# k and q of tiles 9 to 23 transposed by DMA instead of by TensorE, and identity matmuls in TensorE's waits of the first four tiles

## The chip, the cores and the metric

The kernel runs on one core of one Trainium2 chip. The metric is device time in microseconds (us); the kernel before takes 236.11 us, the median of three runs (236.11 to 236.44).

## The reference

Two blocks stand one behind the other. The first is a causal linear attention with a decay per head (4 batches, 8 heads, 768 positions, head size 64), given in blocks of 64 positions:

```python
for b in range(nb):
    ...
    intra = np.einsum('bhic,bhjc->bhij', qb, kb) * Dmask[None]
    intra = np.einsum('bhij,bhjd->bhid', intra, vb)
    inter = np.einsum('bhid,bhde->bhie', qb * lam_pow[None], kv_state)
    out[:, :, sl] = intra + inter
    ...
    kv_state = lam_block[None, :, None, None] * kv_state + np.einsum('bhsd,bhse->bhde', kb_dec, vb)
```

The heads are put side by side to rows of 512. The second block normalizes each row and adds a two-layer network of width 2048:

```python
xn = (x - mu) / np.sqrt(var + 1e-06) * g_ln
ch = np.maximum(xn @ w_ch1, 0.0) @ w_ch2
return (x + ch)
```

Inputs and outputs are float32; the kernel multiplies in bf16.

## The kernel before, in words

The 3072 rows are cut into 24 tiles of 128 positions, six to a batch. The decay is taken out of the mask: q is scaled by lam^(i+1) and v by lam^-(i+1), so that the scores need only a triangular mask, and the state between tiles is multiplied by lam^128. All eight heads of a tile are worked on together, two heads ("a pair") to 128 columns.

A tile goes through these steps.

- `p0` (L293): three loads from HBM on SP's queue (`load_tile`, L56, 256 KB each, in runs of 256 bytes), then three GpSimd instructions: `kb` (k cast to bf16, L138), `qb` and `vb` (q and v scaled, L144 and L146).
- `p1` (L149): TensorE transposes k and q, four 128x128 transposes each (`tk` L153, `tq` L162). ScalarE copies `tk` from PSUM in two halves of 64 partitions (L155, L156) into `kTp`, a buffer whose other halves were zeroed at the start; `qT` is copied by ScalarE for tiles 0 to 3 and by VectorE afterwards.
- `p2` (L170): k transposed times v for the next state (`pk`, L177), its sum with the old state on VectorE (`Stmp`, L184) and the decay on GpSimd (`Sn`, L185); then the scores `sc` (L192), eight 128x128 matmuls whose contraction runs over 128 rows, half of them the zeros of `kTp`, and the mask on VectorE (`mA`, L194).
- `p3` (L198): the output `po` (eight matmuls L203, and four with the state, L207), copied by ScalarE to `x` (L210), its statistics (L212, L214) and the centred, scaled `xc` (L216) on VectorE.
- `p4` (L219): `xc` transposed into `xT`, by TensorE for tiles 0 to 7 (L234) and by a DMA transpose on SP's queue from tile 8 on (L227).
- The two layers work on groups of tiles, of sizes 2, 2, 1, 1, 2, 2, 3, 4, 4, 3 (L288). `m1` (L258) multiplies by the first weights, ScalarE applies the ReLU (L261); `m2` (L271) multiplies by the second weights, VectorE adds x (L282), and SP's queue stores the tile (L284).

Every engine, and SP's queue, works in the order in which the code issues its instructions. Up to group 3 the order is written out by hand (L319 to L370: a list of `units` of the layers, and in `after` the attention steps that follow each). From group 4 on a loop (L388) goes through the units of the layers and hands out attention steps at an even pace, so that the last tile of a group has had its `p4` six units before the group begins. A `round_of(j)` (L306) holds the steps that are taken together. The weights come as eight DMAs issued by GpSimd, `w1` in four (L75) and `w2` in four (L78); the four of `w2` stand in GpSimd's queue behind `vb` of tile 4, which waits for that tile's last load. That load is itself held back by a memset on GpSimd (L63, `after_pool`).

PSUM has two banks `aux` (`tk`, `tq`, `pk`, `xt`), two for scores, one for `po` and three `mm` for the layers.

Of the kernel before, what the change touches and what calls it, by code (L numbers as in the profile page):

```python
# [16 lines left out]
def kernel(  # L17
# [94 lines left out]
    kTp = []  # L112
    for i in range(2):
        kt = const.tile([128, NP, 2, 128], BF16, name=f"kTp{i}")
        nc.vector.memset(kt, 0.0)
        kTp.append(kt)
# [13 lines left out]
    st = {}  # L130
# [4 lines left out]

    def in_k(t, eng):
        kb = wk.tile([128, H, D], BF16, tag="kb", bufs=4, name="kb")
        (eng.copy if eng is nc.scalar else eng.tensor_copy)(kb, qkv_in[t]["k"])  # L138
        st[t] = dict(kb=kb)

    def in_qv(t):
        f = qkv_in.pop(t)
        qb = wk.tile([128, H, D], BF16, tag="qb", name="qb")
        nc.gpsimd.tensor_tensor(qb, f["q"], lam_q[:, :, None].to_broadcast([128, H, D]), op=ALU.mult)  # L144
        vb = wk.tile([128, H, D], BF16, tag="vb", bufs=4, name="vb")
        nc.gpsimd.tensor_tensor(vb, f["v"], lam_v[:, :, None].to_broadcast([128, H, D]), op=ALU.mult)  # L146
        st[t].update(qb=qb, vb=vb)

    def p1(t):  # L149
        s = st[t]  # L150
        tk = ps.tile([128, NP, 128], BF16, tag="aux", bufs=2, name="tk")
        for p in range(NP):
            nc.tensor.transpose(tk[:, p, :], s["kb"][:, 2 * p:2 * p + 2, :], ident)  # L153
        kT = kTp[t % 2]
        nc.scalar.copy(kT[0:64, :, 0, :], tk[0:64, :, :])  # L155
        nc.scalar.copy(kT[64:128, :, 1, :], tk[64:128, :, :])  # L156
        if t < 4:
            tq = ps.tile([128, NP, 128], BF16, tag="mm", bufs=3, name="tq")
        else:
            tq = ps.tile([128, NP, 128], BF16, tag="aux", bufs=2, name="tq")  # L160
        for p in range(NP):
            nc.tensor.transpose(tq[:, p, :], s["qb"][:, 2 * p:2 * p + 2, :], ident)  # L162
        qT = wk.tile([128, NP, 128], BF16, tag="qT", name="qT")
        if t < 4:
            nc.scalar.copy(qT, tq)
        else:
            nc.vector.tensor_copy(qT, tq)  # L167
        s["kT"], s["qT"] = kT, qT

    def p2(t):  # L170
        s = st[t]
        c = t % nb
        s["S"] = state.get("S") if c > 0 else None
        if c < nb - 1:
            pk = ps.tile([128, NP, 128], F32, tag="aux", bufs=2, name="pk")
            for p in range(NP):
                nc.tensor.matmul(pk[:, p, :], lhsT=s["kb"][:, 2 * p:2 * p + 2, :], rhs=s["vb"][:, 2 * p:2 * p + 2, :],  # L177
                                 start=(p == 0), stop=(p == NP - 1), skip_group_check=True)
            Sn = wk.tile([128, NP, 128], BF16, tag="S", name="Sn")
            if c == 0:  # L180
                nc.vector.tensor_tensor(Sn, pk, lamC, op=ALU.mult)
            else:
                tmp = wk.tile([128, NP, 128], F32, tag="Stmp", bufs=2, name="Stmp")
                nc.vector.tensor_tensor(tmp, pk, state["S"], op=ALU.add)  # L184
                nc.gpsimd.tensor_tensor(Sn, tmp, lamC, op=ALU.mult)  # L185
            state["S"] = Sn
        mA = wk.tile([128, H, 128], BF16, tag="mA", name="mA")
        for half in range(2):
            sc = ps.tile([128, H // 2, 128], F32, tag="sc", bufs=2, name="sc")
            for i in range(H // 2):  # L190
                h = half * (H // 2) + i
                nc.tensor.matmul(sc[:, i, :], lhsT=s["kT"][:, h // 2, h % 2, :], rhs=s["qT"][:, h // 2, :],  # L192
                                 start=(i == 0), stop=(i == H // 2 - 1), skip_group_check=True)
            nc.vector.tensor_tensor(mA[:, half * (H // 2):(half + 1) * (H // 2), :], sc,  # L194
                                    tril[:, None, :].to_broadcast([128, H // 2, 128]), op=ALU.mult)
        s["mA"] = mA

    def p3(t):  # L198
# [3 lines left out]
        for h in range(H):  # L202
            nc.tensor.matmul(po[:, h, :], lhsT=s["mA"][:, h, :], rhs=s["vb"][:, h, :],  # L203
# [12 lines left out]
        nc.vector.scalar_tensor_tensor(xc, in0=x, scalar=mv[:, 0:1], in1=g_row, op0=ALU.subtract, op1=ALU.mult)  # L216
# [71 lines left out]
    sizes = [2, 2, 1, 1, 2, 2, 3, 4, 4, 3]  # L288
# [4 lines left out]
    def p0(t):  # L293
        for n in {4: (), 5: (8, 9)}.get(t, (t + 4,)):
            if n < NT:
                load_tile(n)
        in_k(t, nc.gpsimd)
        in_qv(t)
# [20 lines left out]
    for t in range(2):  # L319
        in_k(t, nc.vector)  # L320
        in_qv(t)
# [3 lines left out]
    run((p1, 0), (p2, 0), (p1, 1), (p3, 0))  # L325
    in_k(2, nc.scalar)
    in_qv(2)
    load_w1(0)
    run((p2, 1), (p1, 2), (p3, 1))
    in_k(3, nc.scalar)  # L330
    in_qv(3)
    load_w1(1)
    load_tile(4, after_pool=True)
    run((p2, 2), (p4, 0), (p1, 3), (p3, 2))
    load_w1(2)
    load_w1(3)
    run((p2, 3), (p4, 1), (p0, 4))
# [36 lines left out]
    for j in range(8, NT + 2):  # L374
# [51 lines left out]
```

## Time and profile before

| | |
|---|---|
| median of three runs | 236.11 us |
| the profiled execution, its own time | 235.61 us |
| its span, first to last instruction | 233.9 us |
| TensorE matmuls (PE) busy | 212.4 us, 91% of the span |
| weight loads (PEld) | 136.8 us |
| VectorE (DVE) | 113.3 us, 48% |
| ScalarE (ACT) | 114.3 us, 49% |
| GpSimd (POOL) | 90.1 us, 39% |
| mean granted TensorE clock | 0.981 |
| read from HBM, written | 27.53 MB, 6.29 MB |

In the lines of the profile PE is TensorE's matmuls, PEld its weight loads, SPq the queue of SyncE, which issues the loads, the stores and the DMA transposes. A line of a timeline begins with the start and the length in us. A line of the waits gives the total, the number of times and the longest. The chain is the work that ended last, followed back from the end, each piece released by the one ahead of it. A matmul's duration includes its way through the pipeline, so matmuls that follow each other overlap; what one costs is the distance to the next start.

### The profile page before, as it was taken

How to read it: one execution, taken by the hardware profiler on the slowest of the kernel's cores; microseconds unless marked ns; L12 is line 12 of the kernel's file. 1: busy time of each engine (PE TensorE's matmuls, PEld its weight loads, DVE VectorE, ACT ScalarE, POOL GpSimd, SP SyncE). 2: the span in 40 equal slices, each digit the busy share in tenths (PEclk: the TensorE clock that was granted, in tenths of full speed). 3: DMA queues.
4: the chain of work that ended last, by engine and by line, in shares of the span. 5: the costliest groups of instructions: out<-in, count | busy, mean ns of one | idle time of the engine just before them, and what ended most of it. 6: DMA issues, size and time to landing. Idle time of an engine off the chain costs nothing.

```text
span 233.9 us, 4503 instructions
## 1 busy us (share of the span) xinstructions
PE 212.4 (91%) x1792; PEld 136.8 (58%) x1792; DVE 113.3 (48%) x219; ACT 114.3 (49%) x222; POOL 90.1 (39%) x103
## 2 busy tenths in 40 slices
PE   0664899999999899989999999999999999999992
PEld 0453879644977596579567655555554544456540
DVE  3459530334665567868776656653573223220021
ACT  5765486421546465367437832678213664017400
POOL 2659526216834667952746940633220000000000
PEclk9997799999999999999999999999999999999998
DMA  6998996999999999999999903310011200411012
GB/s 125 221 225 113 221 176 89 182 217 205 225 209 300 204 242 227 209 210 243 168 249 229 160 3 112 93 22 3 34 66 59 67 0 3 125 60 39 3 66 70
DMA packets 91717, 32.02 MB, mean 137 GB/s; under 512 B 84272, under 2 KB 88624, under 8 KB 91696
## 3 DMA queue, kind: packets, MB, share of 16 engines
q1 hardware_dynamic: 87328, 27.53, 58.7%
q0 software_dynamic: 4224, 4.19, 11.3%
q8 instruction: 14, 0.23, 0.4%
q14 instruction: 7, 0.06, 0.1%
q10 hardware_dynamic: 144, 0.00, 0.0%
HBM read 27.53 MB, written 6.29 MB: 145 GB/s over the span
## 4 chain that ended last, share of the span: by engine, by line
PE 70%; DMA 15%; SPq 4%; POOL 4%; DVE 3%; ACT 2%; issue 1%; DVEq 0%; ACTq 0%
PE pm L271 30%; PE pm L258 28%; DMA vin<-in_v_dram 7%; DMA w<-in_moe_w_ch_dram 6%; SPq L65 4%; PE sc L192 3%; PE po L203 2%; DMA xT<-xc 2%; PE tq L162 2%; PE po L207 1%; PE tk L153 1%; POOL vb L146 1%; PE pk L177 1%; DVE xc L216 1%; POOL w L78 1%
## 5 line engine op out<-in xcount | busy, mean ns | idle before, releaser
L258 PE MATMUL pm<-xT,w 128*128 128x256 bf16 (+3 forms) x640 | 90.4, 294 | 1.5 <-DMA xT<-xc 0.8
L271 PE MATMUL pm<-w,hT 128*128 128x512 bf16 x384 | 88.6, 379 | 0.1
L261 ACT ACTIVATE hT<-pm 128x512 bf16<-128x512 f32 (+1 forms) x104 | 58.2, 565 | 44.5 <-PE pm L258 43.6
L258 PEld LDWEIGHTS <-w 128*128 128x128 bf16 x640 | 56.2, 98 | 25.4 <-DMA xT<-xc 1.0
L271 PEld LDWEIGHTS <-hT 128*128 128x128 bf16 x384 | 36.3, 98 | 38.0 <-issue 0.4
L185 POOL TENSOR_TENSOR Sn<-Stmp,lamC 128x512 bf16<-128x512 f32 x16 | 20.4, 1273 | 60.9 <-DVE Stmp L184 60.9
L212 DVE BATCH_NORM_STATS2 stats<-x 128x6 f32<-128x512 f32 x24 | 16.7, 694 | 43.6 <-ACT x L210 43.5
L282 DVE SCALAR_TENSOR_TENSOR o<-pm,rstd,x 128x512 f32<-128x512 f32 (+1 forms) x25 | 18.0, 725 | 33.6 <-PE pm L271 33.3
L194 DVE TENSOR_TENSOR mA<-sc,tril 128x512 bf16<-128x512 f32 x48 | 30.7, 681 | 1.3 <-PE sc L192 1.3
L144 POOL TENSOR_TENSOR qb<-qin,lam_q 128x512 bf16<-128x512 f32 x24 | 25.6, 1066 | 13.7 <-DMA qin<-in_q_dram 13.6
L155 ACT COPY kTp<-tk 64x512 bf16<-64x512 bf16 x24 | 13.7, 572 | 31.4 <-PE tk L153 31.4
L146 POOL TENSOR_TENSOR vb<-vin,lam_v 128x512 bf16<-128x512 f32 x24 | 25.5, 1062 | 3.9 <-DMA vin<-in_v_dram 2.8
L210 ACT COPY x<-po 128x512 f32<-128x512 f32 x24 | 14.0, 585 | 16.0 <-PE po L207 12.5
L216 DVE SCALAR_TENSOR_TENSOR xc<-x,mv,g_row 128x512 bf16<-128x512 f32 x24 | 20.7, 862 | 0.9
L192 PE MATMUL sc<-qT,kTp 128*128 128x128 bf16 x192 | 16.4, 234 | 0.3 <-ACT kTp L156 0.2
L167 DVE COPY qT<-tq 128x512 bf16<-128x512 bf16 x20 | 8.4, 419 | 15.2 <-PE tq L162 15.1
L153 PE MATMUL tk<-ident,kb 128*128 128x128 bf16 x96 | 10.0, 231 | 6.1 <-DVE kb L138 5.5
L138 POOL CAST kb<-kin 128x512 bf16<-128x512 f32 x20 | 13.2, 661 | 5.7 <-DMA kin<-in_k_dram 5.5
L192 PEld LDWEIGHTS <-kTp 128*128 128x128 bf16 x192 | 13.5, 106 | 1.6 <-ACT kTp L156 0.4
L156 ACT COPY kTp<-tk 64x512 bf16<-64x512 bf16 x24 | 13.9, 581 | 0.6
L162 PE MATMUL tq<-ident,qb 128*128 128x128 bf16 x96 | 9.7, 227 | 3.9 <-POOL qb L144 3.5
L203 PEld LDWEIGHTS <-mA 128*128 128x128 bf16 x192 | 9.0, 99 | 6.7 <-DVE mA L194 3.4
(45 smaller groups left out, 112.5 us busy)
## 6 DMA issues: line engine op xcount, KB each, us to landing
kin<-in_k_dram SPq DMA_DIRECT2D x24, 256.0 KB, 4.9
qin<-in_q_dram SPq DMA_DIRECT2D x24, 256.0 KB, 5.0
vin<-in_v_dram SPq DMA_DIRECT2D x24, 256.0 KB, 5.4
out_dram<-o SPq DMA_DIRECT2D x23, 256.0 KB, 2.5
w<-in_moe_w_ch_dram POOLq DMA_DIRECT2D x8, 512.0 KB, 8.0
g_row<-in_moe_g_ln_dram SPq DMA_DIRECT2D x1, 256.0 KB, 5.0
xT<-xc SPq DMA_TRANSPOSE x16, 3.2
out_dram<-o SPq DMA_DIRECT2D x2, 128.0 KB, 1.7
```

Source lines behind the costliest of these rows:

```text
L144: nc.gpsimd.tensor_tensor(qb, f["q"], lam_q[:, :, None].to_broadcast([128, H, D]), op=ALU.mult)
L146: nc.gpsimd.tensor_tensor(vb, f["v"], lam_v[:, :, None].to_broadcast([128, H, D]), op=ALU.mult)
L162: nc.tensor.transpose(tq[:, p, :], s["qb"][:, 2 * p:2 * p + 2, :], ident)
L185: nc.gpsimd.tensor_tensor(Sn, tmp, lamC, op=ALU.mult)
L192: nc.tensor.matmul(sc[:, i, :], lhsT=s["kT"][:, h // 2, h % 2, :], rhs=s["qT"][:, h // 2, :], start=(i == 0), stop=(i == H // 2 - 1), skip ...
L194: nc.vector.tensor_tensor(mA[:, half * (H // 2):(half + 1) * (H // 2), :], sc, tril[:, None, :].to_broadcast([128, H // 2, 128]), op=ALU.mult)
L212: nc.vector.bn_stats(stats, x)
L216: nc.vector.scalar_tensor_tensor(xc, in0=x, scalar=mv[:, 0:1], in1=g_row, op0=ALU.subtract, op1=ALU.mult)
L258: nc.tensor.matmul(pm[:, b, :], lhsT=w1[n // W2K][:, kk, (n % W2K) * 128:(n % W2K + 1) * 128], rhs=xT_of[g][:, kk, 0:N], start=(b == 0 and ...
L261: nc.scalar.activation(hT[:, u * NB:(u + 1) * NB, 0:N], pm, ACT.Relu)
L271: nc.tensor.matmul(acc[i], lhsT=hT[:, kk, i * 128:(i + 1) * 128], rhs=w2[kk // W2K][:, kk % W2K, :], start=(kk == 0), stop=(kk == KB - 1))
L282: nc.vector.scalar_tensor_tensor(o[:, sl], in0=a[:, sl], scalar=rstd, in1=x[:, sl], op0=ALU.mult, op1=ALU.add)
```

## The change

- **Transposes of k and q.** From tile 9 on (`XB = 9`) k and q are written side by side into one buffer `kq` of 128x1024, and one DMA transpose of 256 KB on SP's queue gives `kqT`, which the scores and the state's matmuls read. The eight transposes on TensorE and the three copies from PSUM are gone for these 15 tiles. The DMA transpose is issued one round earlier than `p1` was: `p1(j + 1)` at the start of round j.
- **Scores.** `kTp` with its zeros is gone. `kT` is copied in one instruction, and the eight score matmuls contract over 64 rows each, taking the lower and the upper half of the partitions in turn and writing to two banks in turn.
- **Identity matmuls.** `fill` issues 123 matmuls of the identity with itself during the first four tiles, ahead of the transposes and of the scores. They write to PSUM places that are overwritten right after.
- **Order of the start.** Scores come ahead of the state's step, the state's last multiplication on GpSimd (`fin_state`) is a step of its own, and the first weight DMA is ahead of `vb` of tile 2.
- **The rest.** `xc` reads `po` in PSUM instead of `x`. The groups are 2, 2, 1, 1, 2, 2, 2, 3, 3, 3, 3, so the first layer has 64 more matmuls of the same total width. A tile's loads are issued two `p0` ahead instead of four, and `p4(j - 1)` stands in every round.

```diff
+    XB = 9
     def in_k(t, eng):
-        kb = wk.tile([128, H, D], BF16, tag="kb", bufs=4, name="kb")
+        if t >= XB:
+            kq = wk.tile([128, 2, H, D], BF16, tag="kq", bufs=4, name="kq")
+            kb, qb = kq[:, 0], kq[:, 1]
...
+    def fill(dst, n):
+        for _ in range(n):
+            if dst.dtype == BF16:
+                nc.tensor.transpose(dst, ident, ident)
+            else:
+                nc.tensor.matmul(dst, lhsT=ident, rhs=ident, start=True, stop=True, skip_group_check=True)
+
+    FK, FQ, FS = {0: 40, 2: 8, 3: 6}, {0: 14, 1: 5, 2: 10, 3: 8}, {0: 8, 1: 8, 2: 8, 3: 8}
     def p1(t):
         s = st[t]
+        if t >= XB:
+            kqT = wk.tile([128, 2 * NP, 128], BF16, tag="kqT", name="kqT")
+            nc.sync.dma_start_transpose(kqT, s["kq"].rearrange("p a h d -> p (a h d)"))
+            s["kT"], s["qT"] = kqT[:, 0:NP, :], kqT[:, NP:2 * NP, :]
+            return
         tk = ps.tile([128, NP, 128], BF16, tag="aux", bufs=2, name="tk")
+        fill(tk[:, 0, :], FK.get(t, 0))
...
-        kT = kTp[t % 2]
-        nc.scalar.copy(kT[0:64, :, 0, :], tk[0:64, :, :])
-        nc.scalar.copy(kT[64:128, :, 1, :], tk[64:128, :, :])
+        kT = wk.tile([128, NP, 128], BF16, tag="kT", name="kT")
+        nc.scalar.copy(kT, tk)
...
+    def scores(t):
+        s = st[t]
+        mA = wk.tile([128, 2, NP, 128], BF16, tag="mA", name="mA")
+        sc = [ps.tile([128, NP, 128], F32, tag="sc", bufs=2, name=f"sc{e}") for e in range(2)]
+        fill(sc[0][:, 0, :], FS.get(t, 0))
+        for p in range(NP):
+            for e in range(2):
+                half = slice(e * D, (e + 1) * D)
+                nc.tensor.matmul(sc[e][:, p, :], lhsT=s["kT"][half, p, :], rhs=s["qT"][half, p, :],
+                                 start=(p == 0), stop=(p == NP - 1), skip_group_check=True)
...
-        nc.vector.scalar_tensor_tensor(xc, in0=x, scalar=mv[:, 0:1], in1=g_row, op0=ALU.subtract, op1=ALU.mult)
+        nc.vector.scalar_tensor_tensor(xc, in0=po.rearrange("p h d -> p (h d)"), scalar=mv[:, 0:1], in1=g_row, op0=ALU.subtract, op1=ALU.mult)
...
-    sizes = [2, 2, 1, 1, 2, 2, 3, 4, 4, 3]
+    sizes = [2, 2, 1, 1, 2, 2, 2, 3, 3, 3, 3]
...
     def p0(t):
-        for n in {4: (), 5: (8, 9)}.get(t, (t + 4,)):
-            if n < NT:
-                load_tile(n)
+        if 5 < t < NT - 2:
+            load_tile(t + 2)
...
     def round_of(j):
-        steps = [(p1, j), (p3_p0, j - 1), (p2, j)]
-        if j <= 11:
-            steps.append((p4, j - 1))
-        elif j > 12:
-            steps.append((p4, j - 2))
+        steps = [(p1, j)] if j < XB else []
+        if j + 1 >= XB:
+            steps.append((p1, j + 1))
+        steps += [(p3_p0, j - 1), (p2, j)]
+        steps.append((p4, j - 1))
...
-    run((p1, 0), (p2, 0), (p1, 1), (p3, 0))
+    run((p1, 0), (scores, 0), (next_state, 0), (p1, 1), (scores, 1), (p3, 0), (next_state, 1))
```

SP's queue in group 4, before, from the store of tile 5 on: the loads of tile 15, then the first DMA transpose of the kernel, that of `xc` of tile 8. The loads of tiles 13 and 14 stand ahead of this store.

```order
L284 DMA out_0_dram<-o_1232 128x512
L65 DMA kin_1347<-in_k_dram 128x8x64
L65 DMA qin_1349<-in_q_dram 128x8x64
L65 DMA vin_1351<-in_v_dram 128x8x64
L227 DMA_TRANSPOSE xT_1401<-xc_1345 128x4x128
```

The same queue now, from the store of tile 5 on. `kq_1255`, `kq_1310` and `kq_1458` are k and q of tiles 9, 10 and 11, the loads are those of tile 13, and `xc_1450` is that of tile 8.

```order
L318 DMA out_0_dram<-o_1337 128x512
L166 DMA_TRANSPOSE kqT_1375<-kq_1255 128x8x128
L166 DMA_TRANSPOSE kqT_1419<-kq_1310 128x8x128
L65 DMA kin_1452<-in_k_dram 128x8x64
L65 DMA qin_1454<-in_q_dram 128x8x64
L65 DMA vin_1456<-in_v_dram 128x8x64
L261 DMA_TRANSPOSE xT_1505<-xc_1450 128x4x128
L166 DMA_TRANSPOSE kqT_1521<-kq_1458 128x8x128
```

Two DMA transposes of twice the size stand ahead of the loads, one more stands in every round, and the loads ahead of the transpose of tile 8 are those of tile 13 in place of tile 15: two tiles of loads have moved behind it.

TensorE's queue at the scores of tile 9, before: `kTp1_131` is the padded k, and one bank `sc_1379` takes four matmuls before the next one is begun.

```order
L177 LDWEIGHTS kb_1148
L177 MATMUL pk_1369<-vb_1152,kb_1148 128x128
L192 LDWEIGHTS kTp1_131
L192 MATMUL sc_1379<-qT_1314,kTp1_131 128x128
L192 MATMUL sc_1385<-qT_1314,kTp1_131 128x128
```

The same place now: the weights come from `kqT`, and the matmuls go to `sc0_1483` and `sc1_1484` in turn.

```order
L211 LDWEIGHTS kq_1255
L211 MATMUL pk_1473<-vb_1258,kq_1255 128x128
L198 LDWEIGHTS kqT_1375
L198 MATMUL sc0_1483<-kqT_1375 128x128
L198 MATMUL sc1_1484<-kqT_1375 128x128
```

The number of score matmuls is the same; the transposes `tk` and `tq` of these tiles are no longer anywhere in the queue, and the scores wait for a DMA instead of a copy.

GpSimd's queue from `qb` of tile 2 to the second `w1` DMA and the memset that holds back the loads of tile 4, before:

```order
L144 TENSOR_TENSOR qb_224<-qin_101,lam_q_137 128x512
L146 TENSOR_TENSOR vb_226<-vin_103,lam_v_135 128x512
L75 DMA w1_0_75<-in_moe_w_ch1_dram 128x4x512
L185 TENSOR_TENSOR Sn_234<-Stmp_235,lamC_127 128x512
L144 TENSOR_TENSOR qb_288<-qin_107,lam_q_137 128x512
L146 TENSOR_TENSOR vb_290<-vin_109,lam_v_135 128x512
L75 DMA w1_1_76<-in_moe_w_ch1_dram 128x4x512
L63 MEMSET kin_293 128x1
L185 TENSOR_TENSOR Sn_305<-Stmp_306,lamC_127 128x512
```

And now:

```order
L145 TENSOR_TENSOR qb_315<-qin_101,lam_q_133 128x512
L75 DMA w1_0_75<-in_moe_w_ch1_dram 128x4x512
L149 TENSOR_TENSOR vb_319<-vin_103,lam_v_131 128x512
L219 TENSOR_TENSOR Sn_311<-Stmp_312,lamC_127 128x512
L145 TENSOR_TENSOR qb_405<-qin_107,lam_q_133 128x512
L149 TENSOR_TENSOR vb_408<-vin_109,lam_v_131 128x512
L75 DMA w1_1_76<-in_moe_w_ch1_dram 128x4x512
L219 TENSOR_TENSOR Sn_401<-Stmp_402,lamC_127 128x512
L63 MEMSET kin_412 128x1
```

The first weight DMA is one instruction earlier, and the memset, with it the load of tile 4, is behind the second state multiplication instead of ahead of it.

More of the change, by code (lines that the diff above doesn't have):

```diff
@@ L111 @@
     nc.vector.memset(lamC, 0.0)
[L112 to L116, printed above, removed]
     lnlam = const.tile([128, H], F32)
@@ L373 @@
     steps = []
-    for j in range(8, NT + 2):
+    for j in range(8, NT + 1):
         steps += [s for s in round_of(j) if s not in ((p3_p0, 7), (p4, 7))]
```

65 lines of the change are left out of this document (38 added, 27 removed).

## The prediction

> **What bounds the kernel now.** I read the page first, then the busy time by stretches, TensorE's waits, the chain in order of time, and SP's queue.
>
> ```profile
> PE 212.4 (91%) x1792; PEld 136.8 (58%) x1792; DVE 113.3 (48%) x219; ACT 114.3 (49%) x222; POOL 90.1 (39%) x103
> 31.70:52.00 20.30, 20.24 (x172) 14.67 (x170) 4.27 (x9) 10.26 (x19) 6.66 (x9) 1.00 0.98 159
> 78.70:134.00 55.30, 53.83 (x556) 39.97 (x555) 38.78 (x77) 33.77 (x70) 36.20 (x39) 1.00 1.24 218
> 134.00:229.60 95.60, 95.52 (x611) 49.83 (x609) 35.31 (x69) 39.08 (x76) 13.40 (x14) 1.00 0.16 48
> ```
>
> In the three stretches the first number after the length is TensorE's busy time, and the last two are the share of the DMA engines and GB/s. From 31.7 us on TensorE hardly stops, at full clock. The DMA engines are full too, until 134 us, and nearly idle afterwards. So the kernel is bound by TensorE's work, with a full DMA queue beside it for two thirds of the way. Where one of them is relieved, the other is next.
>
> TensorE's waits, first up to 52 us, then after it:
>
> ```profile
> PE tk L153 <- DVE kb L138: 5.5, 1, 5.5
> PE tq L162 <- POOL qb L144: 3.5, 4, 1.3
> ```
>
> ```profile
> PE xt L234 <- DVE xc L216: 0.9, 1, 0.9
> PE pm L258 <- DMA xT<-xc: 0.8, 1, 0.8
> PE xt L234 <- DVE qT L167: 0.5, 1, 0.5
> PE tq L162 <- DVE Sn L181: 0.4, 1, 0.4
> PE sc L192 <- ACT kTp L156: 0.2, 1, 0.2
> ```
>
> The two longest items of the start are 9.0 us, all of the rest 2.8 us. But the start is not worth what its waits say. The chain between them (start, length, what), and two groups of instructions from the page (busy time, mean of one in ns):
>
> ```profile
> 38.22 13.75 DMA w<-in_moe_w_ch_dram
> ...
> 52.02 4.48 PE pm L271 x20
> ```
>
> ```profile
> L185 POOL TENSOR_TENSOR Sn<-Stmp,lamC 128x512 bf16<-128x512 f32 x16 | 20.4, 1273 | 60.9 <-DVE Stmp L184 60.9
> L192 PE MATMUL sc<-qT,kTp 128*128 128x128 bf16 x192 | 16.4, 234 | 0.3 <-ACT kTp L156 0.2
> ```
>
> TensorE's second layer takes the last quarter of `w2` the moment that it lands, at 51.97 us. A TensorE that is earlier before this point stands there and waits.
>
> **The change, part by part.**
>
> The pieces of the chain from which the costs are taken (start, length, what, how many):
>
> ```profile
> 72.82 0.89 PE pm L258 x16
> 73.71 0.86 PE pm L271 x4
> ...
> 82.13 0.87 PE pm L258 x8
> 83.00 0.22 PE tk L153 x4
> 83.23 0.22 PE tq L162 x4
> 83.45 0.87 PE pm L258 x8
> 84.32 0.23 PE po L203 x8
> 84.56 0.22 PE po L207 x4
> 84.78 0.87 PE pm L258 x8
> 85.65 0.22 PE pk L177 x4
> 85.88 0.45 PE sc L192 x8
> ```
>
> *The first 52 us.* The 123 identity matmuls cost 0.45/8 = 0.056 us each at full clock, 6.9 us in all, and more where the clock is lower. They lie in the waits for `kb` and `qb`, 9.0 us, and in front of the wait for `w2`, which takes up what spills over. If that cover were gone, they would cost their 6.9 us or more. Earlier scores and a warmer clock are worth nothing here for the same reason. What counts is when `w2` is issued. It stands on GpSimd behind `vb` of tile 4, and that tile's load now waits for one more state multiplication (`Sn`, 1.27 us). The price is between 0 and 1.3 us; I take 0, since the load shares its time with the three `w1` DMAs, whose bytes stay the same.
>
> *TensorE after 52 us.* Fifteen tiles lose 0.22 + 0.22 us of transposes: 6.6 us. The scores take 0.45 us for eight; that is one after the other at the pace of 0.056 us. With 64 rows each and the two halves alternating, two could run at once: 0.22 us a tile. No row of this trace has two matmuls side by side. The nearest ones bound it: 0.45 us if they don't overlap (these rows), and 0.23 us for eight pairs of weight load and matmul with 64 columns (`po`), which shows that weight loads can follow at that pace. I take 0.22, a gain of 0.225 us for each of tiles 5 to 23, 4.3 us.
>
> The regrouping adds 64 matmuls at the same total width: eight of 256 columns take 0.87 us, sixteen of 128 take 0.89, so one more start costs 0.0025 us, 0.2 us in all. Of the waits, those for `kTp` (0.2) and for `Sn` ahead of `tq` (0.4) go with their instructions, that for `xT` (0.8) is counted anew below, and 0.9 and 0.5 ahead of `xt` stay: `po`, `x`, statistics and `xc` follow each other as before. So TensorE alone would gain 6.6 + 4.3 - 0.2 + 1.4 = 12.1 us.
>
> The copies that go were off the path: ScalarE and VectorE are busy for less than half of the span. `xc` now holds `po` until it is read, some 2 us longer; the steps of the next tile lie between two `po`, eight pieces of 0.87 us and more in a round of group 4, so nobody waits.
>
> *SP's queue and the DMA engines.* This is where the gain is paid for. Each of 15 tiles adds a DMA transpose of 256 KB into the part in which the DMA engines are full. The rows of the queue:
>
> ```profile
> 53.98 1.80 SPq L65 DMA_DIRECT2D kin<-in_k_dram  x1
> ...
> 64.92 2.01 SPq L65 DMA_DIRECT2D kin<-in_k_dram  x1
> ...
> 69.36 2.54 SPq L284 DMA_DIRECT2D out_dram<-o  x4
> ...
> 80.42 0.38 SPq L65 DMA_DIRECT2D kin<-in_k_dram  x1
> ...
> 130.08 1.92 SPq L227 DMA_TRANSPOSE xT<-xc  x1
> L227 SPq DMA_TRANSPOSE xT<-xc x16: 1191/1518/1924, 92.3 to 203.1; - x16
> DMA to landing us min/median/max: 2.4/3.2/5.9
> ```
>
> In a full queue the pace of issue is the pace of the transfers. From 53.98 to 64.92 us stand nine loads: 1.22 us each. A store takes 2.54/4 = 0.64 us. From 80.42 to 130.08 + 1.92 = 132.0 us stand eleven tiles of loads (33 x 1.22 = 40.3), five stores (3.2) and eight transposes: 51.6 - 43.5 = 8.1 us, 1.0 us for a transpose of 128 KB. At the pace of a load it would be 0.61 us, so each brings 0.4 us of its own (some of it may be SP waiting for `xc`).
>
> No row has a transpose of 256 KB. From below it is a load of the same size, 1.22 us; from above twice the shortest issue of the small one, 2 x 1.19 = 2.4 us. I take 1.22 + 0.4 = 1.6 us, since the 0.4 us look like a cost of each transpose and not of its bytes.
>
> Now the race. TensorE's group 7 needs `xT` of tile 14. Ahead of that one stand, from the first store behind the loads of tile 12 (80.4 us, which the full queue fixes and TensorE doesn't): 5 stores, 8 transposes of k and q, 21 loads and 6 small transposes, 3.2 + 12.8 + 25.6 + 6.0 = 47.6 us. It is issued at 128.0 us and lands 3.2 us later (median of the small ones), at 131.2 us.
>
> ```profile
> 78.71 1.04 PE L258 MATMUL pm<-xT,w 128*128 128x256 bf16 x8
> ```
>
> TensorE begins group 4 at 78.7 - 3 x 0.225 = 78.0 us and does groups 4 to 6 by then: 24 pieces of 0.87 and 24 of 0.86 us (41.5), and of the attention one `tk` and `tq` (0.44), eight `po` (1.8), seven parts with the state (1.5), seven `pk` (1.5) and eight scores at 0.225 (1.8): 48.6 us. It is there at 126.6 us, with 0.4 us of small gaps at 127.0 us, and waits 4.2 us, in one place or in several: the first scores from `kqT` and group 5's `xT` wait for the same queue. Afterwards the rounds are longer and the loads end, so nothing is added.
>
> *The sum*, on the profiled execution: 235.6 - 12.1 + 4.2 = 227.7 us. The median of the runs is 0.5 us over that execution, so the forecast is 228.2 us.
>
> **Pages against rows.** One score matmul takes 234 ns from end to end, at a pace of 56. The Trainium skill says in "TensorEngine Tiling", section Tiling Modes, Key Properties, that a change of the tiling mode drains TensorE. By that rule rival 3 holds; no row here shows such a change. A small transpose takes 1.0 us of the full queue, a load of as many bytes 0.61. The Trainium skill says in "Advanced Engine Details and Errata", section X-Bar Transpose, that transposing DMAs are as fast as plain ones. By that rule rival 2 holds; the 1.0 us speak against it.
>
> **The rivals.**
>
> 1. *The transposes hold the queue up.* If nothing else moves while one is in flight, each costs 3.2 us as from issue to landing. For it: a small transpose already takes 1.6 times what its bytes would. Against: loads and transposes have been mixed from 92 us on without a standstill. Eight of them cost 8 x 1.6 = 12.8 us more than in my sum: 241.0 us, slower than before. It decides from 1.6 + 7.9/8 = 2.6 us a transpose on.
> 2. *The transposes are plain copies.* At 1.22 and 0.61 us the 47.6 us become 42.3, `xT` of tile 14 lands at 125.9 us and TensorE doesn't wait: 224.0 us. For it: when the queue is empty, a small transpose lands in 2.4 us, the least in the row. Against: the 1.0 us.
> 3. *The half-height matmuls drain.* TensorE empties before the first score and after the last: 2 x (0.234 - 0.056) = 0.36 us a tile. For tiles 5 to 15 that goes into the wait for the DMA, for the eight others it is 2.9 us: 231.1 us. Without a drain but without overlap it is 8 x 0.225 = 1.8 us: 230.0 us. No row speaks for or against.
> 4. *The start counts after all*, because `w2` lands earlier. Against: the load of tile 4 is issued later, not earlier. It would take up to 1.3 us off, as much as the move of `Sn` costs at most: 226.9 us.
>
> **How the numbers follow.** The forecast (transposes between 1.25 and 1.95 us, scores overlapped) has a chance of 0.48, rival 2 of 0.20, rival 3 of 0.18, rival 1 of 0.09, rival 4 of 0.05. What can be told from no change is about 0.2%, 0.5 us: from 235.6 to 236.6 us. The forecast's own range, 4.2 us of waiting give or take 8 x 0.35, is 225.4 to 231.0 us. The low end of the range is rival 2 with 1.5 us off, 222.5 us. The high end is a transpose of 2.4 us, 6.4 us more, 234.6 us, set to 235.0. Only rival 1 and rival 3 with dear transposes lie above. Faster: the forecast, rivals 2 and 4, nearly all of rival 3, 0.88. Same: a transpose near 2.6 us, 0.03. Slower: rival 1, 0.09.
>
> **What would show it.** Right: the last quarter of `w2` lands near 52 us and TensorE waits for it; the eight scores stand 0.22 us from start to end of issue; TensorE waits for `kqT` of tile 9 near 85 us and for `xT` of tiles 9 and 14, some 4 to 5 us in all, and for no DMA after about 150 us. The fault would be in the DMA term if these waits are over 10 us or near zero, in the scores if they take 0.45 us or more, and in the first part if `w2` lands more than 1.3 us away from 52 us.

## The result, and the profile after

The changed kernel takes 228.99 us (median of 4 runs, 228.60 to 229.88) against 236.11 us (4 runs, 236.04 to 236.44): a ratio of 0.9701, with a 95% interval from 0.9671 to 0.9731. The forecast was 228.2 us. The profiled execution took 228.60 us, its span is 226.9 us.

The engines on the page, and the busy time in the same three stretches (length, TensorE busy, its weight loads, VectorE, ScalarE, GpSimd, clock, share of the DMA engines, GB/s):

```profile
PE 210.8 (93%) x1859; PEld 136.2 (60%) x1859; DVE 104.3 (46%) x202; ACT 95.6 (42%) x191; POOL 88.1 (39%) x103
```

```profile
31.70:52.00 20.30, 19.91 (x158) 14.36 (x159) 3.94 (x7) 8.24 (x14) 7.01 (x9) 0.92 0.93 154
78.70:134.00 55.30, 54.76 (x513) 37.67 (x514) 33.42 (x65) 22.44 (x44) 30.70 (x33) 1.00 1.12 216
134.00:222.50 88.50, 88.50 (x605) 48.42 (x602) 34.90 (x66) 36.87 (x79) 19.30 (x20) 1.00 0.43 97
```

From 78.7 us on TensorE is idle for 0.5 us in all (most of it in the wait for `xc` shown below, ahead of group 4), although the DMA engines are still full up to 134 us and now carry the transposes of k and q as well. That the wait for the DMA queue did not come is the first thing to explain. The second is the mean clock of 0.92 between 31.7 and 52 us, where it was 1.00 before.

TensorE's waits of the whole span (us in all, times, the longest), and then the only one of them after 52 us:

```profile
PE pm L292 <- DMA w<-in_moe_w_ch_dram: 3.6, 3, 2.7
PE tq L181 <- POOL qb L145: 3.6, 3, 1.6
```

```profile
PE xt L268 <- DVE xc L250: 1.0, 2, 0.8
```

The wait of 5.5 us for `kb` is filled with identity matmuls, but a new one stands in the start: 2.7 us for a quarter of `w1`. No wait for `kqT` or `xT` is left in this execution.

The chain of waits shows where that quarter comes from (start, length, what):

```profile
8.70 6.65 DMA qin<-in_q_dram
15.42 1.04 POOL qb L145
...
22.41 1.25 POOL Sn L219
23.66 8.38 DMA w<-in_moe_w_ch_dram
32.09 10.57 PE pm L292 x80
```

It runs through q of tile 2 and GpSimd's queue to the third quarter of `w1`, which lands at 32.05 us. Behind it 80 matmuls of the first layer take 10.57 us; at 0.109 us each they would take 8.7. The clock says why, in two stretches of 3.41 us (columns as above):

```profile
29.22:32.63 3.41, 0.68 (x8) 0.49 (x6) 0.16 (x1) 1.23 (x3) 0.27 (x1) 1.00 1.22 195
32.63:36.05 3.42, 3.42 (x18) 2.43 (x17) 0.00 (x0) 1.19 (x2) 0.38 (x2) 0.50 1.05 200
```

TensorE worked 0.68 us of the first one, and the second was granted half the clock: 1.7 us of work lost. So the second layer begins at 44.70 us, 2.0 us later than before (42.66).

Group 4 begins at 80.22 us, where the forecast had 78.0. Only 0.2 us of that come from `w1`: the last quarter of `w2`, called `w2[3]` below, landed at 53.59 us, 1.6 us later than before (51.97), and by the records TensorE took it at 53.87 us. A TensorE that had come earlier would have stood there until 53.6 us.

Now the scores of tile 8, from the same chain as the rows shown of before:

```profile
81.70 1.75 PE pm L292 x16
83.45 0.22 PE pk L211 x4
83.67 0.33 PE sc L198 x8
84.00 1.87 PE pm L292 x16
```

The eight scores take 0.33 us instead of 0.45, but the sixteen matmuls behind them take 1.87 us where the sixteen ahead of them take 1.75. What the group gives, its neighbour takes. The starts of the single matmuls in the trace's records, in us:

```
pk  83.452 (the last of four, 0.056 apart)
sc  83.603 83.607 | 83.670 83.673 | 83.726 83.729 | 83.782 83.785
pm  83.933
```

Two and two start 0.003 to 0.004 us apart: the halves do run side by side. But 0.151 us pass from the last `pk` to the first score and 0.148 from the last pair to the next matmul, where 0.056 is the pace: 0.095 and 0.092 us lost at the two changes of height. Nor are weights loaded ahead there: the load for the first score starts at 83.599 us and that for the layer's next matmul at 83.929 us, each 0.004 us before its matmul, where the load for the last `pk` starts 0.054 us before it. From the first `pk` to the matmul behind the scores it is 0.65 us, and was 0.67 (twelve at 0.056).

### The profile page after: what moved, and what is told of

Its sections match the earlier page's. It is cut to its first block, busy times and chain, and to the rows that moved or that the text cites. A ratio compares the mean times of both kernels' runs of the same rounds, so it can differ in the third digit from the quotient of the medians.

```text
span 226.9 us, 4582 instructions
## 1 busy us (share of the span) xinstructions
PE 210.8 (93%) x1859; PEld 136.2 (60%) x1859; DVE 104.3 (46%) x202; ACT 95.6 (42%) x191; POOL 88.1 (39%) x103
## 4 chain that ended last, share of the span: by engine, by line
PE 80%; DMA 7%; SPq 3%; POOL 3%; DVE 3%; issue 1%; ACT 1%; DVEq 0%
PE pm L305 36%; PE pm L292 35%; DMA w<-in_moe_w_ch_dram 4%; DMA qin<-in_q_dram 3%; SPq L65 3%; PE sc L198 3%; PE po L237 2%; PE po L241 2%; PE pk L211 1%; DVE stats L246 1%; POOL qb L145 1%; POOL vb L149 1%; ACT x L244 1%; POOL w L75 1%; DVE xc L250 1%
## 5 line engine op out<-in xcount | busy, mean ns | idle before, releaser
L292 PE MATMUL pm<-xT,w 128*128 128x256 bf16 (+2 forms) x704 | 91.4, 286 | 3.6 <-DMA w<-in_moe_w_ch_dram 3.6
L295 ACT ACTIVATE hT<-pm 128x384 bf16<-128x384 f32 (+1 forms) x112 | 60.1, 537 | 58.8 <-PE pm L292 58.1
L292 PEld LDWEIGHTS <-w 128*128 128x128 bf16 x704 | 63.0, 99 | 26.0 <-DMA w<-in_moe_w_ch_dram 4.2
L250 DVE SCALAR_TENSOR_TENSOR xc<-po,mv,g_row 128x512 bf16<-128x512 f32 x24 | 18.0, 751 | 2.3
L145 POOL TENSOR_TENSOR kq<-qin,lam_q 128x512 bf16<-128x512 f32 x15 | 15.7, 1045 | 1.1 <-DMA qin<-in_q_dram 1.1
L145 POOL TENSOR_TENSOR qb<-qin,lam_q 128x512 bf16<-128x512 f32 x9 | 9.4, 1044 | 15.4 <-DMA qin<-in_q_dram 15.4
L218 DVE TENSOR_TENSOR Stmp<-pk,Sn 128x512 f32<-128x512 f32 x16 | 10.9, 683 | 4.2 <-PE pk L211 4.1
L141 POOL CAST kq<-kin 128x512 bf16<-128x512 f32 x15 | 9.2, 612 | 2.6 <-DMA kin<-in_k_dram 2.6
L237 PE MATMUL po<-vb,mA 128*128 128x64 bf16 x192 | 9.7, 193 | 0.4 <-DVE xc L250 0.3
L271 ACT ACTIVATE std<-mv,eps_t 128x1 f32<-128x1 f32 x24 | 7.0, 293 | 5.4 <-DVE mv L248 5.4
```

What stands on the lines that cost most here:

```text
L145: nc.gpsimd.tensor_tensor(st[t]["qb"], qkv_in[t]["q"], lam_q[:, :, None].to_broadcast([128, H, D]), op=ALU.mult)
L237: nc.tensor.matmul(po[:, h, :], lhsT=s["mA"][:, h % 2, h // 2, :], rhs=s["vb"][:, h, :], start=(h == 0), stop=(not inter and h == H - 1), ...
L250: nc.vector.scalar_tensor_tensor(xc, in0=po.rearrange("p h d -> p (h d)"), scalar=mv[:, 0:1], in1=g_row, op0=ALU.subtract, op1=ALU.mult)
L292: nc.tensor.matmul(pm[:, b, :], lhsT=w1[n // W2K][:, kk, (n % W2K) * 128:(n % W2K + 1) * 128], rhs=xT_of[g][:, kk, 0:N], start=(b == 0 and ...
L295: nc.scalar.activation(hT[:, u * NB:(u + 1) * NB, 0:N], pm, ACT.Relu)
```

## The experiments

Each ratio is that of the kernel to the kernel before the change, measured on the same chip; 0.01 is 2.36 us. The changed kernel stands at 0.9701.

**e1: all transposes of k and q on TensorE.**

```diff
-    XB = 9
+    XB = 24
```

> All k and q are transposed by TensorE again, everything else as changed. Theory (TensorE's work sets the end, the crossbar's transposes are free because the DMA engines are ahead of TensorE by 0.04 to 0.85 us at groups 5 and 7): 15 tiles x 0.44 us come back, 229.0 + 6.6 = 235.6 us, up to 1 us more where TensorE also waits for qT again. Rival (the DMA queue, not TensorE, sets when groups 5 to 7 begin, and the fall came from elsewhere): taking 256 KB a tile out of the queue gives back part of the 6.6 us, 231 to 233 us.

Measured: 235.49 us, ratio 0.9959 (0.9933 to 0.9986), 0.0258 or 6.1 us above the changed kernel. Line 1 of its page:

```profile
PE 217.3 (93%) x1979; PEld 143.6 (61%) x1979; DVE 110.6 (47%) x217; ACT 103.4 (44%) x206; POOL 88.0 (38%) x103
```

TensorE has 120 matmuls and 6.5 us more, and the time rises by 6.1 us (give or take 1 us, from the two intervals). The DMA transposes bring what they take from TensorE, and a cost beside it is not seen; everything else in the change together is worth 0.4% (0.14 to 0.67), about 1 us.

**e4: every transpose of `kqT` issued twice**, the second time into a buffer that nothing reads.

```diff
             nc.sync.dma_start_transpose(kqT, s["kq"].rearrange("p a h d -> p (a h d)"))
+            kqX = wk.tile([128, 2 * NP, 128], BF16, tag="kqX", name="kqX")
+            nc.sync.dma_start_transpose(kqX, s["kq"].rearrange("p a h d -> p (a h d)"))
```

> Each of the 15 DMA transposes of k and q is issued twice, the second time into a buffer that nothing reads. Theory (a transpose of 256 KB takes 1.0 to 1.35 us of the full queue; xT of tile 14 has 0.85 us to spare): eight more ahead of that one land it 8 x 1.0 to 1.35 = 8 to 10.8 us later, TensorE waits 7 to 10 us for xT or kqT: 236 to 239 us. Rival (the queue had room of its own that the doubled transposes fill, since SP and not the engines set its pace): under 4 us of waits, 229 to 233 us.

Measured: 242.04 us, ratio 1.0229 (1.0195 to 1.0262), 12.5 us above the changed kernel by the ratios, more than either expected. Its timeline on TensorE at the first matmuls of groups 5 and 7, with the wait ahead of each in brackets:

```profile
103.80 1.44 PE L294 MATMUL pm<-xT,w 128*128 128x256 bf16 x6 [4.51 <-DMA xT<-xc]
...
141.85 0.81 PE L294 MATMUL pm<-xT,w 128*128 128x384 bf16 x4 [2.95 <-DMA xT<-xc]
```

`xT` of tile 14 lands at 141.71 us instead of 130.43. Group 4 began 0.5 us later here, so eight more transposes took 10.8 us, 1.35 us each, if nothing else held the queue up. (It is open whether the transfer or the issue sets this: SP takes 1.24 us at the least to issue one of them in this run, and 0.57 us at the least for a load of q.) TensorE waits 7.5 us in all for `xT`. The other 4 us are the clock's, in the two stretches behind these waits:

```profile
102.03:108.86 6.83, 5.06 (x24) 3.49 (x24) 0.16 (x1) 1.38 (x3) 2.51 (x3) 0.50 1.12 234
142.99:146.40 3.41, 3.41 (x18) 1.55 (x13) 1.89 (x3) 1.14 (x3) 2.64 (x3) 0.50 1.41 125
```

At half the clock 5.06 and 3.41 us of work cost half of that again, 2.5 and 1.7 us. 7.5 + 2.5 + 1.7 + 0.5 = 12.2 us. The rival, a queue with room to spare, is out. The theory had the waits right and the time too low, because it left the clock out.

**e3: the halves of the scores one after the other.**

```diff
-        for p in range(NP):
-            for e in range(2):
+        for e in range(2):
+            for p in range(NP):
```

> The eight score matmuls of a tile in another order: the four of the lower 64 rows, then the four of the upper ones; the same matmuls with the same two changes of height. Theory (the alternating halves do overlap, 0.225 us for eight, and entering and leaving them costs some 0.2 us that eats the gain): without the overlap a tile takes up to 0.2 us longer, 24 x 0.15 to 0.2 = 3.6 to 4.8 us: 232.6 to 233.8 us. Rival (they never overlap, and the 0.33 us are what eight shorter matmuls take): no change, 229.0 us, the eight stay at 0.33 us.

Measured: 230.10 us, ratio 0.9718 (0.9683 to 0.9753), not to be told from the changed kernel. On its timeline:

```profile
83.66 0.39 PE L211 MATMUL pk<-vb,kb 128*128 128x128 bf16 x4
83.98 0.41 PE L198 MATMUL sc<-qT,kT 64*128 64x128 bf16 x8
84.32 0.28 PE L292 MATMUL pm<-xT,w 128*128 128x256 bf16 x1
```

From `pk` to the next matmul it is 0.66 us, as with alternating halves. My theory failed on its number, but the rival isn't right either: the records have the eight in four pairs again, 0.013 us apart. The two halves overlap in either order of issue, so this order tells nothing of the drain.

This run shows something else. Its kernel does the same work on TensorE and in the queue as the changed one, and yet it waits for `xT` of tile 9, at the first matmul of group 5 (total, times, longest):

```profile
PE pm L292 <- DMA xT<-xc: 1.1, 1, 1.1
```

In the changed kernel `xT` of tile 9 landed 0.04 us before group 5 began (98.73 and 98.77 us). So the wait stayed out there by a margin smaller than what differs between two such kernels.

**e10: `pk` between the scores**, which doubles the changes of height.

```diff
         for p in range(NP):
+            if p == 2 and between:
+                between(t)
             for e in range(2):
...
-        next_state(t)
+        scores(t, between=next_state)
         fin_state(t)
-        scores(t)
```

> In tiles 4 to 23 the four matmuls of the state (pk) stand between the first and the last four score matmuls instead of ahead of all eight; the same matmuls, one more change of height there and back a tile. Theory (each change between 128 and 64 rows costs 0.09 to 0.1 us, since TensorE empties): 19 tiles with pk x 0.19 = 3.6 us more, 232.5 to 233.2 us. Rival (no drain, the 0.1 us ahead of the scores are the loading of two weights or a wait for the copies): no change within 0.5 us, 229.0 to 229.5 us.

Measured: 232.07 us, ratio 0.9832 (0.9804 to 0.9861), 3.1 us above the changed kernel. (Only 16 of these tiles have a `pk`, not 19; the last tile of each sequence needs no new state.) The timeline of the changed kernel, then that of this one, at tile 8:

```profile
82.85 0.60 PE L292 MATMUL pm<-xT,w 128*128 128x256 bf16 x4
83.28 0.39 PE L211 MATMUL pk<-vb,kb 128*128 128x128 bf16 x4
83.60 0.40 PE L198 MATMUL sc<-qT,kT 64*128 64x128 bf16 x8
83.93 0.72 PE L292 MATMUL pm<-xT,w 128*128 128x256 bf16 x5
```

```profile
83.36 0.60 PE L293 MATMUL pm<-xT,w 128*128 128x256 bf16 x4
83.89 0.29 PE L200 MATMUL sc<-qT,kT 64*128 64x128 bf16 x4
84.11 0.40 PE L213 MATMUL pk<-vb,kb 128*128 128x128 bf16 x4
84.44 0.28 PE L200 MATMUL sc<-qT,kT 64*128 64x128 bf16 x4
84.66 0.61 PE L293 MATMUL pm<-xT,w 128*128 128x256 bf16 x4
```

The same sixteen matmuls ahead of the next group take 84.66 - 83.36 = 1.30 us instead of 1.08: 0.22 us for one more change there and back. Sixteen tiles x 0.22 = 3.5 us, and 3.1 came out. The price goes with the change of height, and the rival, no change in the time, is out. Whether TensorE empties there, or only cannot load weights ahead, this run does not separate.

**e2: no identity matmuls.**

```diff
-    FK, FQ, FS = {0: 40, 2: 8, 3: 6}, {0: 14, 1: 5, 2: 10, 3: 8}, {0: 8, 1: 8, 2: 8, 3: 8}
+    FK, FQ, FS = {}, {}, {}
```

> The identity matmuls of tiles 0 to 3 are left out. Theory (the start is set by when w1 and w2 are issued, and GpSimd's steps ahead of w1 wait for loads and not for TensorE): the third quarter of w1 lands at 32.0 us again and TensorE waits for it, no change within 0.5 us: 228.5 to 229.5 us. Rival (the fills keep the clock up, and the first MLP stage pays for it without them): half-clock windows of 3.4 us come back between 13 and 30 us, each costs up to 1.7 us of TensorE's work: 230.5 to 232.5 us.

Measured: 227.71 us, ratio 0.9629 (0.9602 to 0.9655). Both were wrong: the kernel is faster without them, by 0.7% or 1.7 us (give or take 1 us, from the two intervals). Its chain at the same place as above:

```profile
8.66 6.04 DMA qin<-in_q_dram
14.77 1.05 POOL qb L145
```

The load of q of tile 2 takes 6.04 us instead of 6.65, GpSimd's first step behind it begins 0.65 us earlier, and `w1[2]`, the third quarter of `w1`, is issued 0.6 us earlier and lands 1.3 us earlier, at 30.73 us. The delay runs on to `w2`: without the fills the load of tile 4 is issued at 23.17 us instead of 23.77 and `w2[3]` at 39.15 us instead of 40.27, and `w2[3]` lands at 52.95 us instead of 53.59. TensorE had a wait of 1.7 us for `w1[2]` and a stretch at half the clock here too (30.89 to 34.30 us), much as the rival feared, and is still there before `w2[3]` (total, times, longest):

```profile
PE pm L305 <- DMA w<-in_moe_w_ch_dram: 0.3, 1, 0.3
```

It begins group 4 at 79.35 us instead of 80.22. The kernels e1, e3 and e4 have the start of the changed one; in their profiles `w2[3]` lands at 54.17 to 54.47 us and TensorE waits 0.43 to 0.47 us for it, so the profiled execution of the changed kernel is an early one of its kind.

What the fills do to a load is seen among the DMA queues between 12.2 and 13.5 us of the changed kernel (packets, MB, share of 16 engines):

```profile
q8 instruction: 1, 0.02, 5.7%
```

That is a packet of 16 KB of code on one of the sixteen engines, 1.18 us long from 12.30 us on. Without fills the same row is missing here, and the code comes at 21.05 us. 16 KB is as much as this engine's share of a 256 KB load. The Trainium skill says in "Runtime: NRT & Kernel Launch", section Instruction fetch mechanics, that code is refilled in blocks of 16 KiB or 256 instructions; 123 fills are 246 instructions with their weight loads, so the distance fits. It calls the cost mostly hidden; here the load beside it takes longer.

**e8 and e9: one half of the fills each.**

```diff
-    FK, FQ, FS = {0: 40, 2: 8, 3: 6}, {0: 14, 1: 5, 2: 10, 3: 8}, {0: 8, 1: 8, 2: 8, 3: 8}
+    FK, FQ, FS = {2: 8, 3: 6}, {2: 10, 3: 8}, {2: 8, 3: 8}    # e8
+    FK, FQ, FS = {0: 40}, {0: 14, 1: 5}, {0: 8, 1: 8}         # e9
```

> Only the 48 fills of tiles 2 and 3; the 75 of tiles 0 and 1 are left out. Theory (246 more instructions make TensorE's next 16 KB of code load at 12.3 us instead of 21.1, between the loads of tile 2, and that delays q of tile 2 by 0.65 us and all that GpSimd issues behind it): the code load moves to 16 to 19 us, q of tile 2 lands at 14.7 us, 227.5 to 228.2 us. Rival (the fills cost TensorE's own time in front of the state and the copies of tiles 2 and 3): 229 us, q of tile 2 at 14.7 us but w1[2] at 32 us.

> Only the 75 fills of tiles 0 and 1; the 48 of tiles 2 and 3 are left out. Theory (the code load): it stays between 12 and 13 us, q of tile 2 lands at 15.3 to 15.8 us, 228.8 to 229.8 us as with all fills. Rival (TensorE's own time in tiles 2 and 3): w1[2] lands at 30.8 us, 227.7 us as with none.

Measured: e8 229.40 us, ratio 0.9712 (0.9665 to 0.9759); e9 230.02 us, ratio 0.9750 (0.9709 to 0.9790). The load of q behaves as the theory says, though in e8 the code comes at 21.18 us and not at 16 to 19: q of tile 2 takes 6.03 us there, and 6.98 us in e9, where the code comes at 12.61 us. In all fourteen kernels profiled here, the seven with a code load at 12.3 to 13.1 us need 6.65 to 7.05 us for that load, the seven without 5.68 to 6.08 us. (The first seven are also those with the 75 fills of tiles 0 and 1; no run has the one without the other.) But the time of e8 is that of its rival: `w1[2]` is issued at 23.01 us, as in e2, and yet lands at 31.48 us; `w2[3]` lands at 54.14 us, TensorE waits 0.37 us for it, and group 4 begins at 80.53 us. So the code load can explain the first 0.65 us and not the whole 1.7. What holds `w1[2]` and `w2[3]` up in e8 is open; a further code load at 30.98 us stands beside them, 5.9 us earlier than in e2, but no run separates it. e9 has the early code load, and half the clock from 17 to 27 us, but its time goes by `w2[3]` too: it lands at 54.97 us, TensorE waits 0.34 us for it, and group 4 begins at 81.36 us.

**e5: the load of tile 4 ahead of the state multiplication again**, the fills kept.

```diff
     load_w1(1)
-    fin_state(2)
     load_tile(4, after_pool=True)
+    fin_state(2)
```

> The load of tile 4 stands ahead of the state multiplication of tile 2 on GpSimd again, as before the change; the fills and all else stay. Theory (the load of tile 4 sets when w2 is issued, but in the changed kernel TensorE is held up earlier, by w1[2], whose issue this doesn't move): the load is issued 1.3 us earlier and w2 lands 1 to 1.3 us earlier, TensorE gains 0 to 0.5 us: 228.5 to 229.3 us. Rival (the load of tile 4 sets the start): 1.3 us less, 227.7 us.

Measured: 229.27 us, ratio 0.9690 (0.9665 to 0.9715), no difference from the changed kernel. The load is issued 0.9 us earlier, but `w1[2]` lands at 33.01 us and `w2[3]` at 53.86 us, both no earlier. As the theory expected for the time; that `w2` would come 1 us earlier was wrong, so the run does not show what an earlier `w2` is worth. The theory's reason, that `w1[2]` holds TensorE up and `w2` doesn't, fails here: it waits 2.3 us for `w1[2]` and then 0.48 us for `w2[3]`.

**e7, e11, e12, e13: the weights earlier**, all without fills. e7 moves `load_w1(1)` and `load_w1(2)` up:

```diff
     in_q(3)
+    load_w1(1)
     in_v(3)
-    load_w1(1)
-    fin_state(2)
+    load_w1(2)
     load_tile(4, after_pool=True)
+    fin_state(2)
...
-    load_w1(2)
     load_w1(3)
```

> Without the fills, and with the second and third quarter of w1 each issued one GpSimd multiplication earlier (the second ahead of vb of tile 3, the third with the load of tile 4 ahead of the state multiplication). Theory (after 52 us nothing but TensorE counts, and its start is set by when w1[2] and the load of tile 4 come): w1[2] lands 2 to 3 us earlier, the wait of 1.7 us and the half-clock window behind it (1.7 us) go, the second layer starts 2 to 3 us earlier: 225 to 226 us. Rival (the DMA queue binds as soon as TensorE is earlier): waits for xT of tiles 9 or 14 take the place of those for w1, 227.5 us.

e11 is e7 with the load of tile 4 free to go behind that of tile 3 (`load_tile(4)` there, no memset):

> No fills, w1[1] and w1[2] each one GpSimd multiplication earlier, and the load of tile 4 no longer held back by GpSimd: SyncE issues it right behind tile 3, at about 16 us instead of 23 us. Theory (the weights set the start, since the DMA engines are half idle from 20 to 24 us and again from 34 to 36 us): w2 is issued at about 30 us instead of 37 us and its last quarter lands 6 to 8 us earlier; w1[2] stays at 29 to 31 us; the second layer starts at 39 to 42 us instead of 43.4 us: 224.5 to 226 us. Rival (the DMA queue binds as soon as TensorE is earlier): waits of 1 to 3 us for kqT of tile 9, xT of tiles 9 or 14: 226.5 to 227.7 us.

e12 is e7 with two quarters of `w2` between `kb` and `qb` of tile 4; e13 moves the loads of tiles 5 to 7 up behind `w2[1]` as well:

```diff
-    run((next_state, 3), (fin_state, 3), (p0, 4))
-    for c in range(NWC):
-        load_w2(c)
+    run((next_state, 3), (fin_state, 3))
+    in_k(4, nc.gpsimd)
+    load_w2(0)
+    load_w2(1)
+    in_q(4)
+    in_v(4)
+    load_w2(2)
+    load_w2(3)
     load_tile(5, after_pool=True)
```

> The kernel without fills and with w1 earlier (e7), and the first two quarters of w2 issued between kb and qb of tile 4 instead of behind vb. Theory (after the start nothing but TensorE counts; in e7 the second layer waits for w2): w2[0] lands at about 40 us instead of 42.2, the second layer starts at 40.7 us instead of 42.2, w2[3] lands near 50 us: 1.5 to 2 us less than e7, 225.2 to 225.6 us, a ratio of 0.953 to 0.955. Rival (the DMA queue binds, since the loads from tile 5 on keep their time): TensorE meets kqT of tile 9 and xT of tiles 9 and 14 1 to 2 us earlier and waits for them, 226.7 to 227.2 us as e7.

> The same, and the loads of tiles 5 to 7 let go right behind w2[1], some 4 us earlier. Theory: nothing for TensorE but that w2[2] and w2[3] share the engines with three more loads, 225.2 to 226 us. Rival (the DMA queue binds): the queue is 2 to 4 us ahead of TensorE again, the waits for kqT and xT that the kernel without this step has go, 1 to 1.5 us less than that one, 225.2 to 225.8 us against 226.7 to 227.2 us.

Measured, with the places that matter in the profiled execution:

| kernel | w1[2] lands | w2[3] lands | group 4 begins | median | ratio (95%) |
|---|---|---|---|---|---|
| changed | 32.05 | 53.59 | 80.22 | 228.99 | 0.9701 (0.9671 to 0.9731) |
| e2 | 30.73 | 52.95 | 79.35 | 227.71 | 0.9629 (0.9602 to 0.9655) |
| e7 | 29.47 | 52.71 | 79.10 | 227.12 | 0.9612 (0.9573 to 0.9652) |
| e11 | 31.60 | 51.74 | 78.13 | 226.23 | 0.9553 (0.9527 to 0.9579) |
| e12 | 29.10 | 49.17 | 76.03 | 225.19 | 0.9518 (0.9496 to 0.9540) |
| e13 | 29.96 | 50.14 | 76.53 | 225.59 | 0.9540 (0.9521 to 0.9559) |

In every line the median is the start of group 4 plus 148.0 to 149.2 us. Whatever moves the start moves the end by as much. And the start follows `w2[3]`: in e1 to e5, e7 to e9, e11 and e13 TensorE takes this quarter within 0.05 us of its landing, and group 4 begins 26.4 us after it. In the changed kernel and in e12 TensorE comes to it later (26.6 and 26.9 us from landing to group 4); in e10 it waits, and the dearer scores make it 26.9.

e7 gained 1.3 us at `w1` and lost it at `w2`, for which it waits 2.6 us: it can't be told from e2. Its theory (225 to 226 us) failed; the rival's number is nearer, but not for the rival's reason, since only 0.2 us of waits for `xT` are there. In e11 v of tile 4, free to go at 17.53 us, took 17.58 us beside the weights, and `w2`, which stands behind it on GpSimd, was issued at 36.16 us instead of the 30 us expected. So it gained less than the theory had, and not to a wait for the DMA queue, of which there is none. e12 takes `w2` along as expected, and is the best kernel of this study: by its ratio 4.8% below the one before (4.6 to 5.0) and 1.9% below the changed one (1.5 to 2.3). e13 shows no clear difference from it. Both rivals are out. TensorE's timeline in e12, its way into the second layer and at group 7:

```profile
29.58 8.90 PE L292 MATMUL pm<-xT,w 128*128 128x256 bf16 x80
...
40.50 1.03 PE L305 MATMUL pm<-w,hT 128*128 128x512 bf16 x3
```

```profile
127.11 0.81 PE L292 MATMUL pm<-xT,w 128*128 128x384 bf16 x4
```

No wait, full clock, and group 7 begins at 127.1 us, to a tenth the time at which the forecast had TensorE stand there and wait until 131.2. It doesn't wait: `xT` of tile 14 has landed at 126.17 us. The queue has moved along, and these rows of e12 show how, the end of tile 5 on VectorE and then SP's queue:

```profile
76.26 0.73 DVE L316 SCALAR_TENSOR_TENSOR o<-pm,rstd,x 128x512 f32<-128x512 f32 x1
```

```profile
77.02 0.44 SPq L318 DMA_DIRECT2D out_dram<-o  x1
77.55 2.84 SPq L166 DMA_TRANSPOSE kqT<-kq  x2
```

`kqT` of tile 9 stands behind the store of tile 5, and this store waits for TensorE's second layer: it is issued 0.03 us after tile 5 is finished (76.99 us). In the changed kernel tile 5 is finished at 81.18 us, the store is issued at 81.58 and `kqT` at 82.59. GpSimd's casts for `kq` of tile 9 also stand behind TensorE, by way of a state multiplication that waits for `pk`: it begins at 70.61 us in e12 and at 74.80 us in the changed kernel.

## Why the prediction was right, and where it wasn't

The time came out 0.8 us above the forecast, by errors that cancel ahead of group 7: TensorE was 4.3 us later there than forecast (131.28 us instead of 127.0), and the 4.2 us of waiting that the forecast had put there fell away. A TensorE that is up to 4.2 us late only waits less, and the time stays the queue's. That the errors of the scores and of the start came to no more than this is luck.

- **The transposes, -6.6 us: right.** e1 gives 6.1 us, give or take 1.
- **The waits that go, -1.4 us: right.** The three that it names (0.8, 0.4 and 0.2 us) are gone, and from group 4 on TensorE is idle for 0.1 us in all. Ahead of group 4 the two waits for `xc` are left, 1.0 us.
- **The scores, -4.3 us: the step failed that set eight overlapped scores at 0.22 us.** They do overlap, but the starts in the records give a gain of 0.02 us a tile, 0.4 us for 19. Ahead of them 0.095 us are lost and behind them 0.092, which is what the overlap saves. This is the price that rival 3 put on a drain, at half its size: it took 0.36 us for the two, from the time of one matmul from end to end. The Trainium skill's rule ("TensorEngine Tiling (Array Packing)", section Tiling Modes, Key Properties) fits, and the runs give it a number.
- **The start, 0 us: the step failed that took the later issue of `w2` at 0, out of 0 to 1.3 us.** The load of tile 4 was issued 1.9 us later than before (23.77 us instead of 21.86). About 1.3 us of that stand in e2 as well (23.17 us), as much as the state multiplication now ahead of it takes; the other 0.6 us go with the fills and the late q of tile 2. `w2[3]` landed 1.6 us later, beyond the bound. That the wait for it covers what lies ahead was right to 0.2 us: TensorE lost 2.7 us to `w1[2]` and 1.7 to the clock and was 0.2 us late for `w2[3]`, and in e1, e3 and e4 it waited for it. That the fills can cost more than their own 6.9 us of cover, by delaying a load, was not in the sum; e2 puts all fills at 1.7 us.
- **The wait for the DMA queue, +4.2 us: the price was about right, the race wasn't.** I set `kqT` at 1.6 us; e4 measures 1.35, within the bounds. The queue took 45.0 us from the store of tile 5 to the transpose of tile 14 (81.58 to 126.58 us), forecast 47.6, and `xT` of tile 14 landed at 130.43 us, forecast 131.2. But TensorE reached it at 131.28 us and not at 127.0: it began group 4 2.2 us later and gained 1.6 us less at eight tiles of scores; 0.4 us are not accounted for. So it waited 0, not 4.2 us, though narrowly: e3 waited 1.1 us for `xT` and e8 0.5 us for `kqT`. The step that fails deeper is that "the full queue fixes" the start at 80.4 us "and TensorE doesn't". The first store of that stretch holds what TensorE has just made, and in e12, with TensorE 4.2 us earlier, it and the transposes behind it come 4.6 to 5.0 us earlier.
- **Rival 1** (3.2 us a transpose) is out by e4. **Rival 2** (plain copies, 1.22 us) comes near, since 1.35 us is 0.13 above a load; the Trainium skill's sentence on the crossbar ("Advanced Engine Details and Errata", section X-Bar Transpose) fits the 256 KB transposes here far better than the small ones, which the prediction put at 1.0 us against 0.61. **Rival 4** (the start counts) was right that it counts, and had the sign wrong.

So the sum was -12.1 + 4.2 = -7.9 us, and what happened is, on the two profiled executions (235.61 and 228.60), -7.0 us. Group 4 begins 1.5 us later (80.22 instead of 78.71 us). From there on it is 8.5 us less: transposes 6.6, waits 1.4 and scores 0.3 (16 tiles), against 0.2 of regrouping (its term, not tested by itself); 0.4 us are not accounted for.

One thing wasn't tried: a TensorE that is faster after the start, as it would be without the cost at the changes of height. With 0.85 us to spare at tile 14 and 0.04 at tile 9 I expect it to run into the queue at once; no run shows it.

## What to carry to other kernels

Where two queues run neck and neck, find out first whether one of them stands behind the other's results or both behind a common event: what moves that moves both. Here a store on SP's queue waits for TensorE, and TensorE for the last quarter of `w2`. A fill of idle time isn't free because the engine is idle: 123 of them cost 1.7 us here, and a code load among the first loads goes with them. An overlap of small matmuls has to save more than is lost at its two ends. That speaks for many of them behind one change of height (not tried here); and look for the loss in the group behind them, not in their own row.

## What the runs showed of the hardware

- A change between matmuls of 128 and of 64 rows costs 0.09 to 0.10 us each way; within a run of 64-row ones the two halves pair up (0.003 to 0.013 us apart) whether they are issued alternately or four and four. The weight load behind a change starts only 0.004 us before its matmul (e10 and the changed kernel's records).
- Waiting can be paid twice, the second time by the clock. Behind a stretch of 3.41 us with 0.68 us of work the next one ran at half the clock, and in e4 two waits of 4.5 and 3.0 us cost 4.2 us more in this way. It isn't sure to come: e8 waited 2.8 us for `w1[2]` at the same place and kept its clock, and e3 and e5 1.9 and 2.3 us.
- A DMA transpose of 256 KB took 1.35 us of the full queue (e4). SP's issue of one took 1.23 us or more, that of one of 128 KB 1.19 or more, that of a load of q 0.56 or more (changed kernel).
- A 16 KB block of code in the middle of the first loads goes with a load beside it that takes 6.65 to 7.05 us instead of 5.68 to 6.08, 1.0 us more on the mean of seven kernels each.
